# A transformer block on one core: the last 64 features of q and k in 64x64 tiles, a second DMA turn in the attention half, and another order of operations

## The chip, the core and the metric

The kernel runs on one NeuronCore of a Trainium2 chip. The core has a matrix engine (TensorE, PE in the profile, with its weight loads as PEld), three engines for elementwise work (VectorE or DVE, ScalarE or ACT, GpSimd or POOL), and SyncE (SP), which here only issues DMAs. They run side by side and wait for each other by semaphores. PE writes to PSUM, eight banks of 128 partitions by 512 floats, and only DVE and ACT empty these. The metric is the device time of one execution in microseconds; lower is better.

## The reference

Sequence 2048, width 448, batch 1. An attention block with 16 heads of 28 features, in which each position attends to itself and seven earlier positions at distance 2, and then a mixer with a gated MLP; layer norms ahead of each, residuals around each.

```
def _A_ref(x, wqkv, wo):
    H = 16; Dh = D // H
    W, dil = 8, 2
    qkv = (lambda x, *d: x.transpose(*d))((x @ wqkv).reshape(B, S, 3, H, Dh), 2, 0, 3, 1, 4)
    q, k, v = qkv[0], qkv[1], qkv[2]
    ...
    logits = jnp.einsum("bhsd,bhswd->bhsw", q, kg) * scale
    logits = jnp.where(mask[None, None, :, :], logits, -1e9)
    attn = _softmax(logits, axis=-1)
    o = jnp.einsum("bhsw,bhswd->bhsd", attn, vg)
    return (lambda x, *d: x.transpose(*d))(o, 0, 2, 1, 3).reshape(B, S, D) @ wo

def _B_ref(x, w1, w2, w3, w4):
    h = _gelu(_layernorm(x, axis=-1) @ w1)
    ...
    hs = jnp.concatenate([g0, g1, g2, g3], axis=-1) @ w2
    x1 = x + hs
    h2 = _gelu(_layernorm(x1, axis=-1) @ w3) @ w4
    return x1 + h2

h = x + _A_ref(_layernorm(x, axis=-1), A_wqkv, A_wo)
h2 = h + _B_ref(_layernorm(h, axis=-1), B_w1, B_w2, B_w3, B_w4)
```

Here g0 to g3 are the four quarters of h's features, shifted by -1, +1, -2 and +2 positions along the sequence. Everything is bfloat16 with float32 sums in PSUM.

## The kernel before

**Blocks and phases.** The attention half runs over four blocks of 512 rows (index t, four tiles of 128 rows each), the MLP half over five units of 2, 4, 4, 4 and 2 tiles (index u). A phase with its index is a tag: for block t, N1t normalizes, A1t makes q and k, Vt makes v, A2t the products of queries and shifted keys with their sums over features, St the softmax, A3t the weighted sum of values, Ot the output projection with the residual, B1t the second norm, Mt the product with w1 and its gelu. For unit u, B2u is the product with w2, Tu the norm behind it, W3u the product with w3 and its gelu, B3u the product with w4 and the store. The profile writes all of them with one source line, L986, since one helper emits every instruction; groups are told apart by their tiles: `lntm` are normalized rows, `actT` turned rows (features on partitions), `arena` holds weights, q, k and the first mixer product, `qk_r` the query-key products, `bd_r` the block form of the softmax weights, `h3T` the gelu of W3.

**Turning rows.** A product needs its rows with features on the partitions. `TURN` (line 13) says for each block how that is done: "t" by TensorE transposes into PSUM and evictions from there (`transposed`, line 568, and for the first block `transposed_single`, line 589), "d" by one DMA transpose from `lntm` to `actT` on SP's queue (`dma_turn`, line 409). In the attention half it is "ttdd": two blocks by TensorE, two by DMA.

**Two row halves at a time.** The 448 features are cut into chunks of 128 rows at 0, 128, 192 and 320, and the sums run over 64-row halves of them, seven in all. `duo` (line 455) makes two sums at once, in two PSUM banks: matmuls of 64 rows by up to 128 columns alternate between the upper and the lower half of the array, and after half of the work the two sums change places. The second part waits for the end of the first (`sdeps`).

**The last 64 features.** q and k have 448 features each: three groups of 128 and a last one of 64. In A1, the last 64 of q and of k are computed together: POOL gathers their weights side by side into `wr_s` (line 359, filled in `setup_late`, lines 621-622), so that one sum gives 128 columns. The block's 512 rows are split into the two 64-row halves of each tile: bank X has the first halves, bank Y the second, each 128 by 256 with q on the upper 64 partitions and k on the lower. q goes to `qT`, with the first halves on partitions 0-63 and the second on 64-127, and k to `kr[t]` likewise, so four evictions of 64 by 256 follow, and then small ones for the rows that the next window needs. `copy` (line 392) puts an eviction on ACT; unless told otherwise it may be put on DVE instead.

**The order.** Nothing is ordered by the code's sequence. All operations are numbered as they are described, and `ORDER` (line 19) lists the numbers in the order in which they are issued; an engine takes its own operations in that order and waits in it. `OTHER` (line 50) lists the operations that go to their second engine. Waits follow from the data, from reuse of buffers, and from one rule of `arrange`:

```
            if op.insts[0][0] == "dma_start_transpose":
                op.deps.update(turned + moved)
                turned, moved = [op], []
            elif op.is_dma and not callable(op.chan):
                op.deps.update(turned)
                moved.append(op)
```

A DMA transpose waits until the transpose before it and all loads and copies listed since then have landed, and a load or copy waits for the transpose listed last before it. Only the output stores are free of it.

Of the kernel before, what the change touches and what calls it, by code (L numbers as in the profile page):

```python
# [9 lines left out]
F32 = mybir.dt.float32  # L10

_LAST = {}
TURN = {'A1': 'ttdd', 'B1': 'dddd', 'B2': 'tdddd'}
NORM = {'N0': 'vvvv', 'N1': 'avvv', 'B1': 'avvv', 'B2': 'avvvv'}
STATS = {'N1': 'vvva', 'B1': 'avaa', 'B2': 'avvvv'}
NQK, NBD, NLN, NACT, NSM, NO = 3, 4, 2, 4, 1, 6
POWER = {'N1': 'aaaa', 'B1': 'aaaa', 'B2': 'apapp'}
RESIDUAL = 'ttvv'
ORDER = """
# [29 lines left out]
"""  # L49
OTHER = """  # L50
90 94 117 187 447 492 493 505 550 555
"""
FULL = (4,)
FILL = (0, 0, 0, 0)
# [226 lines left out]
def bass_sequential_preLN__sliding_local_dilated__mixer_s_mlp__prompt_kernel(  # L281
    nc, A_x, A_wqkv, A_wo, B_x, B_w1, B_w2, B_w3, B_w4, out,
):
    _, SEQ, D = A_x.shape
# [6 lines left out]
    PADK = 16  # L291
# [6 lines left out]
    S = _Sched()  # L298
# [4 lines left out]
    A_W = A_W3 + 4 * 1792  # L303
# [7 lines left out]
    with ExitStack() as es:  # L311
# [43 lines left out]
        def arv(off, parts, n):  # L355
            return AR[0:parts, off:off + n]

        wqkv_s = arv(A_W, 128, 4 * 1344).rearrange("p (c n) -> p c n", c=4)
        wr_s = arv(A_W + 4 * 1344, 128, 4 * 128).rearrange("p (c n) -> p c n", c=4)
        w3_s = arv(A_W3, 128, 4 * 1792).rearrange("p (c n) -> p c n", c=4)  # L360
        w4_s = arv(A_W, 128, NF * 448).rearrange("p (f n) -> p f n", f=NF)
        qT = arv(A_QG, 128, 4 * QGW).rearrange("p (c n) -> p c n", c=4)
# [29 lines left out]
        def copy(out_ap, in_ap, either=True):  # L392

            if not either:
                return act(out_ap, in_ap, ACT.Copy)
            return S.add("act", "activation", out=out_ap, in_=in_ap, func=ACT.Copy, alts=[("dve", [("tensor_copy", dict(out=out_ap, in_=in_ap))])])
# [56 lines left out]
        TOP, BOT = slice(0, 64), slice(64, 128)  # L453
# [24 lines left out]
        def sums(out, lhsT, rhs, upper):  # L478

            def side(part, chunks):  # L480
                return [(lhsT(c, part), (lambda lo, m, c=c: rhs(c, part, lo, m))) for c in chunks]

            return out, side(TOP, (0, 1, 2, 3) if upper else (0, 1, 3)), side(BOT, (0, 2, 3) if upper else (0, 1, 2, 3))
# [78 lines left out]
        def halves(out, n=4):  # L562
            return lambda v: out(v).rearrange("p (i n) -> p i n", i=n)
# [52 lines left out]
        def setup_late(after):  # L616

            def late(meth, **kw):
                pool(meth, after=after, **kw)

            for lo in (0, 1):
                late("tensor_copy", out=wr_s[:, :, 64 * lo:64 * lo + 64], in_=wqkv_s[:, :, 384 + D * lo:448 + D * lo])
            late("memset", ap=zc[:], constant=0.0)
            for e in range(2):
                late("tensor_copy", out=zc[:, 0:3, e, 16 * e:16 * e + 16], in_=indj[:, 0:3, :])
            late("tensor_copy", out=zc[:, 3, 0, :].rearrange("p (e h) -> p e h", e=2), in_=indj[:, 3:5, :])
            late("memset", ap=onesrow, constant=0.0)
            late("memset", ap=onesrow[0:1, 0:16], constant=1.0)
            late("memset", ap=maskrow, constant=0.0)
            for w in range(1, NW):  # L630
                lo = DIL * (NW - 1 - w)
                late("memset", ap=maskrow[:, 0:64 * w].rearrange("p (r n) -> p r n", n=64)[:, :, lo:lo + DIL], constant=-30000.0)
            late("memset", ap=kk[0][:, :, 0:PADK], constant=0.0)
            late("memset", ap=kr[0][0:64, 0, 0:PADK], constant=0.0)
            late("memset", ap=vw[0:PADK, 0, 0, :], constant=0.0)
            late("memset", ap=gT[:, :, 0:2], constant=0.0)
            late("memset", ap=gT[:, :, 2 + SEQ:4 + SEQ], constant=0.0)
# [30 lines left out]
        def phase_A1(t):  # L668
# [16 lines left out]
            for k in range(0, 6, 2):  # L685
# [2 lines left out]
                ev_a()  # L688
                ev_b()
            X, Y = _Tile(P_bank), _Tile(P_bank)  # L690

            def half(b, at, upper):
                return sums(lambda lo, n: b(halves(lambda v: v[:, 0:256])), lambda c, part: wr_s[part, c, :],
                            lambda c, part, lo, n: a(lambda v: v[part, :, c, at:at + 64]), upper)

            def last(b, lo, n):
                return b(lambda v: v[64:128, 0:256].rearrange("p (j n) -> p j n", j=4)[:, lo:lo + n, 64 - PADK:])

            duo(half(X, 0, True), half(Y, 64, False), ((0, 256),))
            for h, b in enumerate((X, Y)):  # L700
                copy(qT[64 * h:64 * h + 64, 3, now:now + 256], b(lambda v: v[0:64, 0:256]))
                copy(kr[t][64 * h:64 * h + 64, :, PADK:], b(lambda v: v[64:128, 0:256].rearrange("p (j n) -> p j n", j=4)), False)
            copy(kr[t][64:128, :, 0:PADK], last(X, 0, 4), False)
            copy(kr[t][0:64, 1:4, 0:PADK], last(Y, 0, 3), False)
            if t + 1 < NST:
                copy(kr[t + 1][0:64, 0:1, 0:PADK], last(Y, 3, 1), False)
                copy(kk[t + 1][:, :, 0:PADK], kk[t][:, :, 512:KVW])

        def phase_V(t):
# [318 lines left out]
```

## Time and profile before

| | us |
|---|---|
| median of 3 runs | 190.22 |
| range of these runs | 189.76 to 191.77 |
| the profiled execution | 191.08 |
| its span | 189.4 |
| PE busy | 180.2 |
| DVE busy | 129.1 |
| ACT busy | 121.7 |
| POOL busy | 27.7 |

The span is the time from the first to the last instruction that the profiler recorded; 1.7 us of the execution lie around it. Busy time is the union of an engine's instructions; PE's includes matmuls that overlap, so it doesn't say how near PE is to its peak. The granted TensorE clock is 1.00 throughout. In the tables of the profile, a group's line has its source line, engine, operation, written tile <- read tiles, shape and count, then busy us and mean ns of one, then the engine's idle time just before these instructions and what ended it. The page's slices show the two halves of the kernel: DVE and ACT are full for the first part and have room afterwards, while PE is full throughout.

```profile
PE   6899999998998999999799999999999999999994
DVE  6999999999999979999996503963945320100602
ACT  3489999989999799986299397053365014640340
DMA  5991056856905555620932400514007210000213
```

Each digit is a fortieth of the span, 4.7 us, in tenths of busy time.

### The profile page before, as it was taken

Reading aid. Unit: us, or ns where it says so; the run is one execution under the profiler, and the core shown is the slowest. Engines: PE = TensorE matmul, PEld = TensorE weight load, DVE = VectorE, ACT = ScalarE, POOL = GpSimd, SP = SyncE. Lnnn points to the kernel's source line nnn. Section 1 sums busy time; section 2 is a strip of 40 time slices with the busy share of each in tenths; the row PEclk is TensorE's granted clock in tenths of the full one; section 3 lists DMA queues with packets and bytes.
Section 4 is the critical chain, followed back from the end, with each engine's and each line's share of the span. In section 5 each row is a group of like instructions: output and inputs, shape, how many; then the busy total and the mean of one; then the engine's idle time right before and its main releaser. Section 6 shows DMA issues by size and latency. Waiting matters only on the chain.

```text
span 189.4 us, 5659 instructions
## 1 busy us (share of the span) xinstructions
PE 180.2 (95%) x2450; PEld 97.5 (51%) x2450; DVE 129.1 (68%) x227; ACT 121.7 (64%) x293; POOL 27.7 (15%) x61
## 2 busy tenths in 40 slices
PE   6899999998998999999799999999999999999994
PEld 2584433453443654675345455565445554555773
DVE  6999999999999979999996503963945320100602
ACT  3489999989999799986299397053365014640340
POOL 4330000000000000018705000044040660000000
PEclk9999999999999999999999999999999999999999
DMA  5991056856905555620932400514007210000213
GB/s 154 331 294 36 16 111 158 196 102 149 249 1 114 99 171 208 156 78 0 116 83 32 86 0 3 113 37 102 0 18 167 51 37 22 0 3 0 91 60 97
DMA packets 32161, 17.70 MB, mean 93 GB/s; under 512 B 20888, under 2 KB 31624, under 8 KB 32136
## 3 DMA queue, kind: packets, MB, share of 16 engines
q1 hardware_dynamic: 32136, 17.34, 38.1%
q8 instruction: 19, 0.31, 0.7%
q14 instruction: 6, 0.05, 0.1%
HBM read 7.91 MB, written 1.84 MB: 51 GB/s over the span
## 4 chain that ended last, share of the span: by engine, by line
PE 66%; ACT 16%; DVE 8%; DMA 7%; issue 1%; SPq 0%
PE ps L986 66%; DMA actT<-lntm 6%; ACT arena L986 5%; ACT lntm L986 5%; ACT actT L986 3%; ACT vt L986 2%; DVE lntm L986 2%; DVE st L986 2%; DMA xin<-in_A_x_dram 1%; DVE bd_r L986 1%; DVE arena L986 1%; SPq L986 0%; DVE ls L986 0%; DVE mx L986 0%; ACT rs_x L986 0%
## 5 line engine op out<-in xcount | busy, mean ns | idle before, releaser
L986 PE MATMUL ps<-actT,arena 64*128 64x512 bf16 (+1 forms) x756 | 69.8, 329 | 2.0 <-DMA actT<-lntm 1.4
L986 ACT ACTIVATE h3T<-ps 128x512 bf16<-128x512 f32 (+1 forms) x70 | 30.6, 521 | 34.7 <-PE ps L986 34.4
L986 PEld LDWEIGHTS ps<-actT,arena 64*128 64x128 bf16 x756 | 36.2, 94 | 31.4 <-PE ps L986 2.6
L986 PE MATMUL ps<-arena,h3T 64*128 64x448 bf16 (+2 forms) x434 | 45.6, 343 | 0.0
L986 ACT ACTIVATE arena<-ps 128x512 bf16<-128x512 f32 (+6 forms) x71 | 32.2, 491 | 5.5 <-PE ps L986 4.8
L986 DVE SCALAR_TENSOR_TENSOR qk_r<-ps,mrs,arena 128x448 bf16<-128x448 f32 (+1 forms) x17 | 10.7, 652 | 33.7 <-PE ps L986 33.7
L986 PEld LDWEIGHTS ps<-arena,h3T 64*128 64x128 bf16 (+1 forms) x434 | 24.2, 94 | 18.0 <-ACT h3T L986 0.2
L986 DVE TENSOR_TENSOR qk_r<-arena 128x4096 bf16<-128x4096 bf16 (+1 forms) x16 | 32.0, 2013 | 0.0
L986 POOL TENSOR_TENSOR arena<-arena,xin 128x448 f32<-128x448 f32 x16 | 16.7, 1072 | 28.1 <-DVE lntm L986 28.1
L986 DVE TENSOR_TENSOR bd_r<-arena,bmask 80x2048 bf16<-80x2048 bf16 x16 | 19.1, 1213 | 0.0
L986 POOL TENSOR_TENSOR rs_y<-rs_x,mhalf 128x4 f32<-128x4 f32 (+1 forms) x3 | 2.8, 919 | 86.5 <-DVE rs_x L986 86.5
L986 DVE SCALAR_TENSOR_TENSOR arena<-xin,rs_y,ps 128x448 f32<-128x448 bf16 x16 | 10.4, 673 | 6.6 <-PE ps L986 6.5
L986 ACT ACTIVATE lntm<-xin,nm 128x448 bf16<-128x448 bf16 x16 | 10.6, 663 | 6.5 <-DVE nm L986 6.5
L986 PE MATMUL ps<-wo_s,actT 64*128 64x448 bf16 x128 | 14.3, 350 | 0.4 <-ACT actT L986 0.2
L986 PE MATMUL ps<-actT,w_s 64*112 64x512 bf16 x112 | 13.0, 377 | 1.1 <-DMA actT<-lntm 1.1
L986 PE MATMUL ps<-w_s,arena 64*128 64x448 bf16 (+1 forms) x128 | 13.7, 349 | 0.1
L986 ACT ACTIVATE actT<-ps 128x512 bf16<-128x512 f32 (+2 forms) x20 | 12.1, 640 | 1.5 <-PE ps L986 1.4
L986 PE MATMUL ps<-arena,actT 64*128 64x448 bf16 x112 | 12.6, 350 | 0.1
L986 PEld LDWEIGHTS ps<-actT,w_s 64*112 64x112 bf16 x112 | 7.6, 127 | 6.1 <-DMA actT<-lntm 1.6
L986 ACT ACTIVATE rs_x<-mv,epsilon 128x4 f32<-128x4 f32 (+2 forms) x16 | 4.6, 293 | 9.2 <-DVE mv L986 9.1
L986 DVE TENSOR_SCALAR lntm<-xin,nm,rs_y 128x512 bf16<-128x512 bf16 x13 | 4.7, 404 | 8.5 <-ACT rs_y L986 8.5
L986 DVE TENSOR_SCALAR lntm<-arena,mv,rs_y 128x512 bf16<-128x512 f32 x14 | 8.1, 635 | 2.6 <-POOL rs_y L986 2.0
(72 smaller groups left out, 162.1 us busy)
## 6 DMA issues: line engine op xcount, KB each, us to landing
arena<-in_B_w_dram SPq DMA_DIRECT2D x2, 896.0 KB, 6.1
out_dram<-qk_r SPq DMA_DIRECT2D x15, 112.0 KB, 2.0
arena<-in_B_w_dram SPq DMA_DIRECT2D x2, 784.0 KB, 5.2
vw<-vt SPq DMA_DIRECT2D x4, 320.0 KB, 4.8
vw<-vt SPq DMA_DIRECT2D x4, 256.0 KB, 4.3
arena<-in_A_wqkv_dram SPq DMA_DIRECT2D x2, 448.0 KB, 4.4
xin<-in_A_x_dram SPq DMA_DIRECT2D x2, 448.0 KB, 7.0
xin<-in_A_x_dram SPq DMA_DIRECT2D x3, 224.0 KB, 5.3
```

The lines of the kernel that those rows point to most:

```text
L986: inst = getattr(eng, meth)(**kw)
```

## The change

1. In A1, the last 64 features are computed in tiles of 64 rows by 64 columns. Bank X now is q alone and bank Y k alone, each 128 by 256: the first 64-row halves of the tiles on partitions 0-63, the second on 64-127. So four matmuls belong together, one for each quarter of the array: two row halves for the two sums and two column halves for the two halves of the rows. Weights are read from `wqkv_s` directly. Seven such steps make 28 matmuls of 64*64 with 256 columns in a stage, in two groups of 16 and 12, where there were 14 of 64*128, in groups of 8 and 6.
2. Each bank is emptied by one eviction of 128 partitions by 256, and k's may now be put on DVE too. The small evictions stay.
3. `wr_s` and the two POOL copies that fill it are gone.
4. `TURN['A1']` is 'tddd': the second block's rows are turned by a DMA on SP's queue. Its 32 transposes, in four groups, and the two evictions behind them are gone.
5. `ORDER` and `OTHER` are new: 846 numbers instead of 861, and ten operations on their second engine, as before, but others.

```
-TURN = {'A1': 'ttdd', 'B1': 'dddd', 'B2': 'tdddd'}
+TURN = {'A1': 'tddd', 'B1': 'dddd', 'B2': 'tdddd'}
...
-            for lo in (0, 1):
-                late("tensor_copy", out=wr_s[:, :, 64 * lo:64 * lo + 64], in_=wqkv_s[:, :, 384 + D * lo:448 + D * lo])
...
-            def half(b, at, upper):
-                return sums(lambda lo, n: b(halves(lambda v: v[:, 0:256])), lambda c, part: wr_s[part, c, :],
-                            lambda c, part, lo, n: a(lambda v: v[part, :, c, at:at + 64]), upper)
...
-            duo(half(X, 0, True), half(Y, 64, False), ((0, 256),))
-            for h, b in enumerate((X, Y)):
-                copy(qT[64 * h:64 * h + 64, 3, now:now + 256], b(lambda v: v[0:64, 0:256]))
-                copy(kr[t][64 * h:64 * h + 64, :, PADK:], b(lambda v: v[64:128, 0:256].rearrange("p (j n) -> p j n", j=4)), False)
+            both = ((X, D - 64, ((0, 1, 2, 3), (0, 2, 3))), (Y, 2 * D - 64, ((0, 1, 3), (0, 1, 2, 3))))
+            op = None
+            for second in range(2):
+                turned = [op] * second
+                specs = []
+                (bu, wu, cu), (bl, wl, cl) = both[::-1] if second else both
+                for n, (ct, cb) in enumerate(zip(cu[0], cl[1])):
+                    for e in range(2):
+                        for b, w, c, part in ((bu, wu, ct, TOP), (bl, wl, cb, BOT)):
+                            specs.append((e, dict(out=b(lambda v, e=e: v[64 * e:64 * e + 64, 0:256].rearrange("p (i n) -> p i n", i=4)),
+                                                  lhsT=wqkv_s[part, c, w:w + 64], rhs=a(lambda v, e=e, c=c, part=part: v[part, :, c, 64 * e:64 * e + 64]),
+                                                  start=not second and n == 0, stop=bool(second) and n == 2), 256))
+                op = S.group("pe", [("matmul", kw) for _, kw, _ in specs], pe=[(n, "s", None) for _, _, n in specs])
+                op.sdeps.update(turned)
...
+            copy(qT[:, 3, now:now + 256], X(lambda v: v[:, 0:256]))
+            copy(kr[t][:, :, PADK:], Y(lambda v: v[:, 0:256].rearrange("p (j n) -> p j n", j=4)))
```

The first numbers of the old and of the new list:

```
-0 1 39 40 41 42 43 44 6 45 46 47 48 49 5 2 33 8 34 7 9 29 36 10 50 51 12 37 30 13 52 55 56 62 57 53 14 3 58 60 61 63
+8 3 29 9 0 33 1 39 40 41 42 43 44 45 10 46 47 7 5 50 2 55 6 51 48 62 56 57 36 52 60 49 61 58 53 63 54 59 87 64 65 89
```

Where the new list is counted off against the phases, these differences matter for what follows. SP's queue starts with the loads of x and of wqkv as before; then come the second block's DMA turn, a copy of V0's last rows, two loads of wo, another copy of V0, the third block's turn, and only then the remaining loads. DVE takes the first query-key product of A2 in block 0 ahead of the statistics of block 2, which stood ahead of it. Of the evictions that a second engine may take, DVE loses one of A10's turned rows, the small one of q in A10 and one of A13, and takes one more in A32 and one more in A33; of B10's normalizations it takes two instead of one. M1 follows M0 on PE with one group of block 2's softmax between them, and the groups of V3 and A13 that stood there stand ahead of M0. B10's and B11's turns are still neighbours on SP's queue, with a load of w3 and a copy of V2's rows behind them. Three groups of A33 and all of O3 stand behind the first group of M2 on PE, and A33's block products stand behind B12's normalizations on DVE. The attention half's exponentials, logarithms and the gelus change places on ACT ten times instead of eight.

More of the change, by code (lines that the diff above doesn't have):

```diff
@@ L19 @@
 ORDER = """
[29 rows of a table removed]
[28 rows of a table added]
 """
 OTHER = """
-90 94 117 187 447 492 493 505 550 555
+88 182 183 374 477 478 484 490 534 541
 """
@@ L358, in bass_sequential_preLN__sliding_local_dilated__mixer_s_mlp__prompt_kernel @@
         wqkv_s = arv(A_W, 128, 4 * 1344).rearrange("p (c n) -> p c n", c=4)
-        wr_s = arv(A_W + 4 * 1344, 128, 4 * 128).rearrange("p (c n) -> p c n", c=4)
         w3_s = arv(A_W3, 128, 4 * 1792).rearrange("p (c n) -> p c n", c=4)
@@ L690, in phase_A1 @@
             X, Y = _Tile(P_bank), _Tile(P_bank)
-            def half(b, at, upper):
-                return sums(lambda lo, n: b(halves(lambda v: v[:, 0:256])), lambda c, part: wr_s[part, c, :],
-                            lambda c, part, lo, n: a(lambda v: v[part, :, c, at:at + 64]), upper)
-            def last(b, lo, n):
-                return b(lambda v: v[64:128, 0:256].rearrange("p (j n) -> p j n", j=4)[:, lo:lo + n, 64 - PADK:])
-            duo(half(X, 0, True), half(Y, 64, False), ((0, 256),))
@@ L700, in phase_A1 @@
-            for h, b in enumerate((X, Y)):
-                copy(qT[64 * h:64 * h + 64, 3, now:now + 256], b(lambda v: v[0:64, 0:256]))
-                copy(kr[t][64 * h:64 * h + 64, :, PADK:], b(lambda v: v[64:128, 0:256].rearrange("p (j n) -> p j n", j=4)), False)
-            copy(kr[t][64:128, :, 0:PADK], last(X, 0, 4), False)
-            copy(kr[t][0:64, 1:4, 0:PADK], last(Y, 0, 3), False)
+            both = ((X, D - 64, ((0, 1, 2, 3), (0, 2, 3))), (Y, 2 * D - 64, ((0, 1, 3), (0, 1, 2, 3))))
@@ L705, in phase_A1, with last @@
+            def last(lo, h, n):
+                return Y(lambda v: v[64 * h:64 * h + 64, 0:256].rearrange("p (j n) -> p j n", j=4)[:, lo:lo + n, 64 - PADK:])
+            copy(qT[:, 3, now:now + 256], X(lambda v: v[:, 0:256]))
+            copy(kr[t][:, :, PADK:], Y(lambda v: v[:, 0:256].rearrange("p (j n) -> p j n", j=4)))
+            copy(kr[t][64:128, :, 0:PADK], last(0, 0, 4), False)
+            copy(kr[t][0:64, 1:4, 0:PADK], last(0, 1, 3), False)
             if t + 1 < NST:
-                copy(kr[t + 1][0:64, 0:1, 0:PADK], last(Y, 3, 1), False)
+                copy(kr[t + 1][0:64, 0:1, 0:PADK], last(3, 1, 1), False)
```

55 rows, old and new, of the table ORDER are left out of this document.

## The prediction

> **What bounds the kernel now.** I read the busy time of each engine in stretches first, then the chain of waits to see where the stretches end, then the groups by form for prices, then the timeline around the places that the change touches.
>
> ```profile
> 12.40:34.40 22.00, 21.36 (x273) 9.68 (x269) 22.00 (x28) 21.73 (x59) 0.00 (x0) 1.00 0.45 93
> 34.40:61.80 27.40, 25.19 (x506) 11.94 (x506) 26.59 (x38) 26.69 (x71) 0.00 (x0) 1.00 0.58 134
> 61.80:94.40 32.60, 31.02 (x516) 18.17 (x518) 31.21 (x53) 25.20 (x56) 8.00 (x8) 1.00 0.50 120
> 94.40:186.90 92.50, 92.42 (x1066) 51.88 (x1066) 38.58 (x83) 42.28 (x94) 14.51 (x16) 1.00 0.22 49
> ```
>
> Columns: stretch, its length, then busy time (instructions) of PE, weight loads, DVE, ACT, POOL, granted clock 1.00, DMA. Three engines are full together until 61.8, and DVE fullest: 22.00 of 22.00. After 94.4 PE alone is full, and it stays so.
>
> ```profile
> 12.42 1.08 ACT arena L986 x2
> ...
> 15.08 1.83 ACT actT L986 x2
> ...
> 55.81 5.94 DMA actT<-lntm
> ...
> 88.86 5.46 DMA actT<-lntm
> ...
> 94.37 92.46 PE ps L986 x1066
> ```
>
> The chain (start, duration, what) names ACT from 12.42 on, though DVE has no gap there either: of two full engines the chain can show only one. Its last pieces are the frame of my sum. DVE normalizes the second unit of the second half (T1), a DMA turns its rows, W31 starts at 94.37, and PE then runs 92.46 us without a wait. The end moves with W31's start, with PE's work behind it, and with waits that appear there.
>
> **The change, part by part.** *Evictions.* Each of the four stages gives up two of its four 64-partition evictions of the last features, and the second block gives up the two evictions of its transposes.
>
> ```profile
> L986 ACT ACTIVATE h3T<-ps 128x256 bf16<-128x256 f32 x28 | 8.7, 395 | 11.9 <-PE ps L986 11.8
> L986 ACT ACTIVATE arena<-ps 64x256 bf16<-64x256 f32 x15 | 5.7, 377 | 0.3
> L986 ACT ACTIVATE actT<-ps 128x1024 bf16<-128x1024 bf16 x2 | 2.0, 1052 | 0.0
> L986 DVE COPY actT<-ps 128x512 bf16<-128x512 bf16 x3 | 1.3, 418 | 0.2 <-PE ps L986 0.2
> L986 DVE CAST actT<-ps 128x512 bf16<-128x512 f32 x1 | 0.7, 692 | 0.0
> L986 DVE CAST arena<-ps 128x512 bf16<-128x512 f32 x1 | 0.7, 680 | 0.0
> L986 DVE CAST arena<-ps 64x256 bf16<-64x256 f32 x1 | 0.4, 382 | 0.0
> L986 DVE TENSOR_SCALAR lntm<-xin,nm,rs_y 128x512 bf16<-128x512 bf16 x13 | 4.7, 404 | 8.5 <-ACT rs_y L986 8.5
> ```
>
> An eviction of 128 partitions by 256 takes 0.395 us and one of 64 by 256 takes 0.377, so eight calls go for 8 x 0.377 less 8 x 0.018, or 2.9 us, and with the two of 1.05 it is 5.0 us. All of it is ACT's (one of the small ones stood on DVE). ACT's share is worth something only where ACT is what DVE and PE wait for, so I book none of it by itself.
>
> *DVE up to T1.* Here the new order has to be read. Counting the new list off against the phases, DVE's queue up to T1's last normalization loses a copy of A10 (0.42), the small q copy (0.38) and one eviction of A13 (0.68), which all go to ACT; it gains a normalization of B10 (0.40) and an eviction of A32 (0.69). It also puts two operations of S3 behind T1 that stood ahead of it.
>
> ```profile
> 84.25 0.69 DVE L986 TENSOR_REDUCE mx<-ps 128x64 f32<-128x512 f32 x1
> 84.97 0.69 DVE L986 TENSOR_TENSOR ls<-ps,mx 128x512 f32<-128x512 f32 x1
> ```
>
> Sum: -0.42 - 0.38 - 0.68 + 0.40 + 0.69 - 2 x 0.69 = -1.8 us. If DVE stays full, T1's turn is issued at 88.86 - 1.8 = 87.1 and lands, after the same 5.46, at 92.5. The first product of A20 now stands ahead of the statistics of N12, but that only swaps two pieces of a full engine.
>
> *PE up to W31.* The turn is one condition, PE's own arrival the other.
>
> ```profile
> 91.87 1.49 PE L986 MATMUL ps<-arena,h3T 64*128 64x448 bf16 x14
> 94.37 6.43 PE L986 MATMUL ps<-actT,arena 64*128 64x512 bf16 x58 [1.01 <-DMA actT<-lntm]
> 61.80 3.23 PE L986 MATMUL ps<-actT,w_s 64*112 64x512 bf16 x28 [1.09 <-DMA actT<-lntm]
> ```
>
> PE ended its earlier work at 91.87 + 1.49 = 93.36 and then waited 1.01 for the turn; it had waited 1.09 for B10's turn ahead of M0. The prices of what changes:
>
> ```profile
> L986 PE MATMUL ps<-actT,arena 64*128 64x256 bf16 x336 | 21.1, 269 | 0.5 <-DVE bmask L986 0.2
> L986 PE MATMUL ps<-qk_r,zc 128*32 128x512 bf16 x112 | 8.1, 383 | 0.0
> L986 PE MATMUL ps<-ident,lntm 64*128 64x64 bf16 x48 | 1.2, 190 | 0.0
> ```
>
> The busy time over the count is what one instruction adds while others overlap it. The 32 transposes of the second block: 1.2/48 = 25 ns each, -0.8 us. The last features: now 56 matmuls at 21.1/336 = 63 ns, 3.5 us; then 112 of half the columns of weights. No 64x64 tile stands in the trace. Below, the pace of the small transposes, 25 ns, gives 2.8 (-0.7). Above, halves that do not overlap cost 63 each, 7.1 (+3.5). I take the row nearest in kind, the products with column tiles (zc): 8.1/112 = 72 ns for 512 columns, four in flight, so 36 ns for 256: 4.0 us, +0.5.
>
> The eight groups are also a new shape among 64-by-128 ones.
>
> ```profile
> 38.89 0.92 PE L986 MATMUL ps<-arena,actT 64*128 64x448 bf16 x8
> 39.65 0.92 PE L986 MATMUL ps<-wo_s,actT 64*128 64x448 bf16 x8
> 47.66 0.93 PE L986 MATMUL ps<-arena,actT 64*128 64x448 bf16 x8
> 48.52 0.42 PE L986 MATMUL ps<-bd_r,vw 80*32 80x64 bf16 x32
> ```
>
> From start to start eight matmuls took 0.76 us ahead of a group of their own shape and 0.86 ahead of one with column tiles: 0.10 for a change of shape. In the new order the eight groups add eleven such changes (five of sixteen edges touch each other or a column-tiled group that PE would have switched for anyway): +1.1. [...] With shape changes free, PE's sum would be -0.3 instead of +0.8, and W31 would wait for its turn until 92.5.
>
> So PE's work ahead of W31 changes by -0.8 + 0.5 + 1.1 = +0.8. Against it stands the wait of 1.09 at M0: the new order puts fourteen matmuls of V3 and six of A13 ahead of M0 that stood behind it, about 1.7 us (14 at 0.76/8 = 95 ns, 6 at 63), and B10's normalizations stand behind the same DVE work as now. So PE is still busy when that turn lands. PE arrives at 93.36 + 0.8 - 1.09 = 93.1, behind the turn's 92.5. W31 starts at 93.1, which is 1.3 earlier.
>
> *The turned block.* The new DMA stands on SP's queue behind the loads of x. Its issue waits for all of them, and the loads of wo and one wait for V0's rows queue behind it; the next block's turn stands behind those.
>
> ```profile
> xin<-in_A_x_dram SPq DMA_DIRECT2D x2, 448.0 KB, 7.0
> actT<-lntm SPq DMA_TRANSPOSE x10, 4.4
> 5.26 1.38 SPq L986 DMA_DIRECT2D xin<-in_A_x_dram  x2
> 11.76 1.31 DVE L986 TENSOR_SCALAR lntm<-xin,mv,rs_y 128x448 bf16<-128x448 bf16 x4 [0.47 <-ACT rs_y L986]
> 17.07 4.19 PE L986 MATMUL ps<-actT,arena 64*128 64x512 bf16 x42
> ```
>
> The rows are normalized at 13.1; the last load, issued at about 6.2, lands at 13.2 (7.0 later). With 4.4 the turned rows are there at 17.6, 0.5 behind the 17.07 of now; between the loads' contention and an idle queue I keep 16.5 to 19.2 (5.94, the longest above). PE gets V0 and the first product there; DVE, the fullest engine, has the other products of A20 and the statistics of N12 as cover. I cost it at 0; without that cover it is 0.5 to 2.1. The two gathers of weights by POOL, which is idle from 12.4 to 61.8, go for nothing.
>
> *Behind that.* Two places lose cover. M1 follows M0 with little between them, where V3, A13 and B20 stood, and its turn starts only when B10's has landed: 0 to 1.5 us, most of it ahead of W31's other condition. All of O3 (32 matmuls at 95 ns, 3.0 us) and three groups of A33 now stand behind M2's first group, so PE asks for B12's turn that much sooner; DVE's four block products of A33 stand behind B12's normalizations in return: 0 to 1. I take +0.3 for both. ACT gets one more pair of table loads around M3, where it is less than half busy (42.28 of 92.50): 0.
>
> Sum: -1.3 + 0.3 = -1.0 us. The profiled execution took 191.08 us, span 189.4 and 1.7 around it, 0.86 above the median of 190.22. So 190.1 for it, and **189.2** by the median.
>
> **The rivals.**
>
> *The column halves don't overlap (slower).* For it: no row shows two row tiles and two column tiles at once, and twice as many weight loads must hide. [...] Against: four column tiles did overlap (72 ns per 512 columns). Then a matmul costs 63 instead of 36 ns, PE's sum is +3.8 instead of +0.8, W31 starts at 96.1, 1.7 later than now, and with the 0.3 the median is 192.2. It turns slower than before from about 45 ns per matmul: (1.0 + 4.0)/112.
>
> *Nothing reaches the end.* DVE's 1.8 us turn into waits, because its inputs come from PE, which has 0.8 more to do, or from the late turn (2.1 above). For it: the three engines are full together, and relief went to ACT. Against: the two operations of S3 need nothing new to stand behind T1. The median stays at 190.2. That the order simply trades equal pieces is the same case.
>
> *The whole relief counts (faster).* ACT is on the chain from 12.42 on, and 1.83 of its 5.0 us stand in it as one piece. If DVE and PE had been paced by ACT, W31 starts up to 3 us earlier: 187.2. Against: DVE's 22.00 of 22.00.
>
> **How the numbers follow.** Forecast 0.45, halves apart 0.17, nothing reaches the end 0.23, whole relief 0.15. A difference under 1% (1.9 us) is what I call no change. Below 188.3 lies the whole-relief case and a quarter of the forecast's spread (the turn alone would allow 1.8 or more, and the matmuls may cost 25 ns): 0.27. Above 192.1 lie most of the halves case and a part of the late turn together with a lost cover: 0.17. The rest is 0.56. Ends: 187.0, the whole relief, and 192.2, the halves; what goes beyond is left out.
>
> **What would show it.** 112 matmuls of 64*64 at about 36 ns by busy time over count; ACT's busy time near 118 us with DVE's near 129; T1's normalizations ending near 87 and W31 starting near 93, with PE waiting there for no turn; no wait of PE above 1 us at M1, M2, M3 and W32; M0 starting without a wait. I am wrong if W31 starts later than 94.4, or if PE shows waits of over 1 us in total behind it.

## The result and the profile after

The changed kernel took 189.71 us in the median of 19 executions, the kernel before 190.94 in 19 beside them: a ratio of 0.9946, 95% interval 0.9921 to 0.9971. A second measurement (12 executions, first experiment) gave 189.61 and 0.9949 (0.9924 to 0.9973). So it is faster by about 0.5%, 1.0 us. Four of these 31 executions have a mean granted clock of 0.990 or 0.991 and took 191.7 to 192.2; the ratios leave out the three slowest and so aren't the quotients of the medians. The first profile caught the fourth (191.67), with the clock at half for 3.4 us. I therefore read the profile of the second measurement: 189.96 us, span 188.2, clock 1.00, beside 191.08 and 189.4 before.

The end of its chain of waits (start, duration, what):

```profile
62.21 4.28 DMA actT<-lntm
66.51 0.38 SPq L990
66.94 8.46 DMA vw<-vt
75.45 2.76 PE ps L990 x136
78.41 107.32 PE ps L990 x1304
185.75 0.45 DVE qk_r L990
```

Before, the last pieces were T1's normalizations, its turn, and PE from W31 on. Now PE runs without a wait from 78.41, and T1's turn is no longer in the chain: it is issued at 87.42 and has landed by 92.55, when the next DMA, which waits for it, is issued.

```profile
87.42 3.18 SPq L990 DMA_TRANSPOSE actT<-lntm  x1
92.55 0.62 SPq L990 DMA_DIRECT2D vw<-vt  x1
```

The waits of PE on the way there, and W31 (timeline; in brackets the idle time and its releaser):

```profile
38.21 0.70 PE L990 MATMUL ps<-bd_r,vw 80*32 80x64 bf16 x64 [1.11 <-DVE lntm L990]
...
63.20 2.54 PE L990 MATMUL ps<-actT,w_s 64*112 64x512 bf16 x22
...
75.45 0.99 PE L990 MATMUL ps<-bd_r,vw 80*32 80x64 bf16 x96 [0.56 <-DMA vw<-vt]
...
93.08 7.07 PE L990 MATMUL ps<-actT,arena 64*128 64x512 bf16 x64
```

M0 (63.20) and W31 (93.08) start without the 1.09 and 1.01 that stood there. In their place there is a new wait of 1.11 at A30. It is put down to a DVE normalization, which this group doesn't read; in the first profile the same wait is 1.66 and its releaser is the copy of V0's rows (vw<-vt). Another wait, of 0.56, is for V2's rows, which stand behind B11's turn on SP's queue.

The kernel before and then the changed one, in two stretches up to W31 (length, then busy time of PE, weight loads, DVE, ACT and POOL with instructions, granted clock, DMA share, GB/s):

```profile
12.40:61.80 49.40, 46.54 (x779) 21.62 (x775) 48.59 (x65) 48.43 (x128) 0.00 (x0) 1.00 0.52 116
61.80:94.37 32.57, 31.00 (x514) 18.14 (x515) 31.18 (x53) 25.17 (x56) 8.00 (x8) 1.00 0.50 120
```

```profile
12.40:61.80 49.40, 46.98 (x809) 21.11 (x803) 48.53 (x66) 44.49 (x122) 0.00 (x0) 1.00 0.55 122
61.80:93.08 31.28, 30.36 (x510) 18.41 (x506) 28.74 (x53) 25.33 (x59) 17.32 (x10) 1.00 0.59 138
```

ACT gave up 3.9 us ahead of 61.8; DVE is as full as ever there. From 12.40 to W31 PE's busy time went from 77.54 to 77.34 and its idle time from 4.43 to 3.34: together the 1.29 by which W31 starts earlier.

### The profile page after: what moved, and what is told of

Its sections match the earlier page's. It is cut to its first block, busy times and chain, and to the rows that moved or that the text cites. A ratio compares the mean times of both kernels' runs of the same rounds, so it can differ in the third digit from the quotient of the medians.

```text
span 190.0 us, 5698 instructions
## 1 busy us (share of the span) xinstructions
PE 181.6 (96%) x2474; PEld 99.8 (53%) x2474; DVE 127.2 (67%) x227; ACT 119.2 (63%) x285; POOL 33.9 (18%) x59
## 4 chain that ended last, share of the span: by engine, by line
PE 80%; DMA 9%; DVE 5%; issue 2%; SPq 2%; ACT 1%
PE ps L990 80%; DMA vw<-vt 4%; DVE qk_r L990 3%; DMA arena<-in_A_wqkv_dram 3%; DMA actT<-lntm 2%; SPq L990 2%; ACT arena L990 1%; DVE st L990 1%; DVE lntm L990 1%; DVE mx L990 0%; DVE mv L990 0%; DVE nm L990 0%; SPq L988 0%
## 5 line engine op out<-in xcount | busy, mean ns | idle before, releaser
L990 PE MATMUL ps<-actT,arena 64*128 64x512 bf16 (+2 forms) x812 | 69.5, 326 | 1.2 <-DMA arena<-in_A_wqkv_dram 0.5
L990 PEld LDWEIGHTS ps<-actT,arena 64*128 64x128 bf16 (+1 forms) x812 | 38.0, 96 | 28.9 <-issue 2.1
L990 ACT ACTIVATE arena<-ps 128x512 bf16<-128x512 f32 (+6 forms) x65 | 29.5, 506 | 8.6 <-PE ps L990 8.3
L990 POOL TENSOR_TENSOR mrs<-nm,rs_y 128x4 f32<-128x4 f32 x4 | 9.7, 2436 | 54.5 <-ACT rs_y L990 54.5
L990 PE MATMUL ps<-wo_s,actT 64*128 64x448 bf16 x128 | 15.2, 364 | 0.1
L990 PE MATMUL ps<-arena,actT 64*128 64x448 bf16 x112 | 13.7, 366 | 0.2
L990 ACT ACTIVATE actT<-ps 128x512 bf16<-128x512 f32 (+1 forms) x17 | 9.4, 600 | 4.1 <-PE ps L990 4.0
L990 DVE BATCH_NORM_STATS2 st<-xin 128x6 f32<-128x448 bf16 x16 | 9.0, 613 | 1.6 <-DMA xin<-in_A_x_dram 1.6
L990 ACT ACTIVATE vt<-ps 128x448 bf16<-128x448 f32 x16 | 8.7, 551 | 2.0 <-PE ps L990 1.9
L990 PEld LDWEIGHTS ps<-wo_s,actT 64*128 64x128 bf16 x128 | 6.3, 97 | 6.9 <-PE ps L990 0.9
```

The costliest lines, as they stand in the source:

```text
L990: inst = getattr(eng, meth)(**kw)
```

## The experiments

All are orders or code of these two kernels with one thing altered. In diffs of an order only the neighbours of what moved are shown.

**The changed kernel again** (a_again), unaltered.

> The changed kernel, unaltered. In its profiled execution the granted clock stood near 0.5 from 40 to 43.4 us and the span was 190.0; other executions had the clock at 1.00 and spans of 187.2 to 188.4. My theory (the low clock is an accident of some executions, and costs about 2 us where it falls): executions at clock 1.00 take 189.0 to 190.1 us, any at 0.99 take 191.5 to 192.2; in a profile at clock 1.00 W31 starts at 92.0 to 93.1 without a wait of PE, T1's normalizations end at 86.5 to 87.5, and DVE has no gap of 0.9 and 1.5 us between 41 and 45. Rival (the low clock costs nothing, something else makes the long executions long): spans of both kinds at clock 1.00.

189.61 us. Eleven executions at clock 1.00 took 189.03 to 190.36, the one at 0.991 took 191.95. My theory holds, but for the 190.36, which lies above its 190.1. W31 starts at 93.08 without a wait, at the late end of what I expected, T1's normalizations end at 87.2, and the gaps of 0.9 and 1.5 us on DVE are gone.

**The parts in the old order.** The tiles alone (b_tiles): the change to the code of A1's tail, none to TURN or the sequence, apart from the numbers that disappear. The turn alone (b_turn):

```diff
-TURN = {'A1': 'ttdd', ...
+TURN = {'A1': 'tddd', ...
```

Both (b_both): the two together, still in the old sequence.

> The kernel before with the 64x64 tiles alone: its order kept, the two gathers and eight small evictions left out. My theory (ACT's relief is worth nothing by itself, only DVE's queue and PE's arrival count): DVE gives up one eviction of 0.38, PE takes on 112 x 41 ns less 56 x 63 ns = 1.1 us and some changes of shape (up to 1.6) of which up to 2.1 us fall into its waits ahead of M0 and W31: -0.4 to +0.6 us, ratio 0.998 to 1.003. Rival (ACT paced the first 60 us): ACT gives up 2.5 us ahead of M0, ratio 0.985 to 0.992. Rival (the new tiles cost more than their waits hide): ratio above 1.005.

> The kernel before with the second block turned by DMA alone: its order kept, but the turn stands on SP's queue ahead of the first two loads of wo. My theory (DVE is full and has cover, the turn lands at 17.6 instead of the rows being there at 17.07): 0 to +0.5 us, ratio 1.000 to 1.003. Rival (ACT's 1.83 us in the chain of waits at 15.08 counts): ratio 0.990 to 0.993. Rival (the late rows reach DVE): +0.5 to +2.1 us, ratio 1.003 to 1.011.

> The kernel before with both changes to the code, the 64x64 tiles and the turn by DMA, in its old order. Theory A (the old order has no use for ACT's relief, so the parts' prices add up; the tiles alone gave +1.4 and the turn alone +0.5): 191.4 to 192.4 us. Theory B (ACT's relief counts once it is large enough, 5.0 us): 188.0 to 189.8 us.

Tiles 191.84 us, ratio 1.0062 (1.0028 to 1.0095); turn 190.89, 1.0020 (0.9994 to 1.0046); both 192.23, 1.0072 (1.0045 to 1.0098). The turn alone came out as expected. For the tiles alone the third case came in, which I hadn't favoured; its profiled execution (190.88) lies below its own median and doesn't show what the others lost. For b_both, theory A held: the two prices add up, and in its profile T1's normalizations start at 86.08, no earlier than the 85.58 before, so no gain from ACT's relief shows on DVE.

The profiles of these three runs show one thing more. T1's turn lands 4.27 us after its issue in each of them, instead of 5.46, and W31 starts at 92.93 (tiles), 92.53 (turn) and 93.70 (both), earlier than the 94.37 before. After its first 16 matmuls PE then waits 0.82 us for a bank that DVE empties. In the old order an early turn alone therefore meets this bank as the next condition.

**The new order without the parts.** Either part undone in the changed kernel: the 64x128 tiles back (a_oldtail; each extra eviction directly behind the one it belonged to), the transposes back (a_oldturn; where the DMA stood), and both (a_order). In a second try the transposes stand directly behind the last normalization (a_oldturn2).

> The new order alone: the last features in 64x128 tiles with four evictions of 64 partitions and the two gathers, the second block turned on TensorE, everything in the new order (the eight extra evictions behind the ones they belonged to). Theory A (the order alone brings the gain: on DVE's queue T1's normalizations no longer meet the two additions of POOL, so its turn is out of the way, and PE's new arrangement does the rest): 189.0 to 190.0 us, the same as the changed kernel. Theory B (the new order lives on the relief of ACT, 5.0 us, since it hands ACT three copies more; without it ACT is late and PE waits): 190.6 to 193 us, with new waits of PE for ACT's evictions ahead of M0.

> The changed kernel with the 64x128 tiles for the last features again (four evictions of 64 partitions, two gathers), the second block still turned by DMA. Theory A (PE paces from 78 us on, and the small tiles cost it 112 x 41 less 56 x 63 ns = 1.1 us): 188.5 to 189.4 us, faster than the changed kernel. Theory B (ACT's 2.9 us are needed by the new order): 190.0 to 191.5 us.

> The changed kernel with the second block turned on TensorE again (32 transposes and two evictions of 1.05 us on ACT), the 64x64 tiles kept. Theory A (the turn by DMA gains nothing, its rows come 0.5 us later instead): 189.3 to 190.0 us. Theory B (PE's 0.8 us and ACT's 2.1 us count): 190.4 to 192.5 us.

> As the changed kernel with the second block turned on TensorE, but with the 32 transposes and their two evictions directly behind the block's last normalization in the order, and not where the DMA stood (there the evictions stood behind ACT's work for the third block, and PE idled 3.85 us for them). Theory A (what the turn by DMA takes off, PE's 0.8 us and ACT's 2.1 us, is used by the new order): 190.4 to 192.1 us. Theory B (only the place of the evictions cost time): 189.3 to 190.0 us.

All four are slower, as theory B says, and each by more than its range. As a table, with the ratio to the kernel before:

| code | old order | new order |
|---|---|---|
| old | 190.4 to 191.3 (1) | 197.79 (1.0334) |
| 64x64 tiles | 191.84 (1.0062) | 195.65 and 195.60 (1.0215, 1.0237) |
| turn by DMA | 190.89 (1.0020) | 194.31 (1.0168) |
| both | 192.23 (1.0072) | 189.61 (0.9949) |

The old code is the kernel before, given as its medians beside the different runs. Where PE waits in the new order without the parts (a_order):

```profile
24.67 4.26 PE L985 MATMUL ps<-actT,arena 64*128 64x512 bf16 x22 [5.22 <-ACT actT L985]
39.29 0.49 PE L985 MATMUL ps<-ident,pb 64*80 64x64 bf16 x16 [1.19 <-ACT arena L985]
```

and with the turn by DMA but the old tiles (a_oldtail):

```profile
20.54 1.69 PE L985 MATMUL ps<-actT,arena 64*128 64x512 bf16 x14 [1.06 <-ACT arena L985]
...
32.77 0.49 PE L985 MATMUL ps<-ident,pb 64*80 64x64 bf16 x16 [0.88 <-ACT arena L985]
```

In a_order PE waits for evictions by ACT, and the clock stands at 0.50 for 6.8 us, which is part of the loss (see the end). In a_oldtail, whose profiled execution took 192.99 us at clock 1.00 throughout, these waits explain little: PE starts the transposes of T0's rows at 77.31, where the changed kernel starts them at 77.26. Of the 3.1 us by which its span is longer (191.3 and 188.2), 2.8 are one wait behind that:

```profile
80.63 0.61 PE L985 MATMUL ps<-qk_r,zc 128*32 128x512 bf16 x8 [2.79 <-issue]
```

"issue" means that the profile shows nothing that PE waited for; the cause stays open. What goes from the code is mostly ACT's time, worth nothing in the old order, and the new order has handed ACT other work in its place. That it stands only with that time free is my reading, which the waits for ACT support where the turn is put back (5.22 us in a_order, 3.85 in a_oldturn), and which isn't shown for the tiles. The places of the put-back operations are mine; another search might lose less. a_oldturn2 shows at least that the late transposes of a_oldturn weren't its only trouble.

**Two tiles or four in flight** (a_halves).

```diff
-                for n, (ct, cb) in enumerate(zip(cu[0], cl[1])):
-                    for e in range(2):
+                for e in range(2):
+                    for n, (ct, cb) in enumerate(zip(cu[0], cl[1])):
```

> The changed kernel with the 28 matmuls of each stage's last features issued one column half after the other instead of alternating, so that at most two tiles are in flight. Theory A (the alternation is what brings 41 ns apiece): 55 to 65 ns apiece by busy time over count, 1.6 to 2.7 us more of PE, 190.5 to 192.2 us. Rival (the order within the group doesn't matter): 41 ns and 189.6 us.

189.50 us, 4.8 us for the 112 matmuls, 43 ns apiece: my theory fell. The single starts in the trace say why (us; one group in the second half of its run, the changed kernel and a_halves):

```
alternating:      30.303 30.306 30.309 30.383   30.412 30.415 30.419 30.491
half after half:  30.699 30.727 30.750 30.758   30.808 30.836 30.859 30.867
```

Four start every 0.108 us in both. Two tiles alone would give two: of the 64*128 tiles with the same 256 columns, which alternate between the upper and the lower half, two start every 0.109 us in the kernel before (78.056 and 78.060, then 78.166 and 78.169). So matmuls of the second half seem to start ahead of earlier ones of the first. The trace doesn't name the half of a start, but the distances fit: in a_halves the second pair of a group starts 26 to 31 ns behind the first where eight matmuls of one half are listed first, and 20 where six are, about 3.3 ns for each matmul in between, as between neighbours; with alternation it is 7. The pace is 27 ns, and the 41 of busy time over count hold the run-out of short groups.

**T1's normalizations and POOL** (b_pool). DVE's part of the new order, first the kernel before, then the changed one:

```profile
85.58 3.25 DVE L986 TENSOR_SCALAR lntm<-arena,mv,rs_y 128x512 bf16<-128x512 f32 x4
```

```profile
85.30 1.91 DVE L990 TENSOR_SCALAR lntm<-arena,mv,rs_y 128x512 bf16<-128x512 f32 x4 [0.92 <-POOL rs_y L990]
```

The same four instructions take 1.34 us less. What ran beside them on POOL, before and after:

```profile
85.42 2.21 POOL L986 TENSOR_TENSOR arena<-arena,xin 128x448 f32<-128x448 f32 x2
```

```profile
76.85 2.03 POOL L990 TENSOR_TENSOR arena<-arena,xin 128x448 f32<-128x448 f32 x2 [4.55 <-ACT lntm L990]
```

These are T0's additions. The experiment moves nothing but them, in the kernel before (550 and 549 are T0's normalizations, 610 T1's reciprocal roots):

```diff
-... 550 ... 549 ... 610 ... 552 ... 551 ...
+... 550 ... 549 551 552 ... 610 ...
```

> The kernel before with one change of order: the two additions that POOL does for T0 stand directly behind T0's normalizations, and no longer beside T1's. Theory A (POOL's additions, which run from 85.4 to 87.6 in the kernel before, are what stretches T1's four normalizations to 3.25 us; in the changed kernel they take 1.91 us): 1.8 to 2.1 us for the four, T1's turn issued at 87.3 to 87.8, no wait of PE at W31's first matmul, and 0.3 to 1.0 us off the time, since a wait for a bank may follow at the next group. Rival (the additions slow DVE's work at 77 to 79 us by as much): T1's normalizations begin 1 us later, the time as before.

189.97 us, ratio 0.9955 (0.9929 to 0.9980). DVE and PE of this run:

```profile
85.46 1.91 DVE L986 TENSOR_SCALAR lntm<-arena,mv,rs_y 128x512 bf16<-128x512 f32 x4
```

```profile
93.36 6.43 PE L986 MATMUL ps<-actT,arena 64*128 64x512 bf16 x58 [0.65 <-DMA actT<-lntm]
```

Theory A held in duration and time, and the rival fell: the additions now run at 76.69, and T1's normalizations begin at 85.46, no later than before. The wait at W31 didn't go, though: the turn was issued at 87.40 as expected but took 5.9 us to land instead of the 5.5 and 5.1 of the other two, and no wait for a bank came behind it. With no change to the code, this one move gives as much as the whole change, within the intervals.

**The wait at A30.** Two ways to free V0's copies (129, 130). Ahead of the third block's turn (321), a_vw:

```diff
-... 236 131 231 ... 321 242 22 ... 129 ... 23 ... 130 ...
+... 236 131 129 130 231 ... 321 242 22 ... 23 ...
```

and behind that turn, but ahead of the last two loads of wo (22, 23), a_wo:

```diff
-... 321 242 22 ... 129 ... 23 ... 130 ...
+... 321 242 ... 129 ... 130 22 23 ...
```

> The changed kernel with V0's two large copies of rows issued ahead of the third block's turn instead of behind it. Theory A (PE's idle time at 37 to 39 us, which is a wait for these copies, lets the clock fall, and the wait itself costs nothing because DVE is the fuller engine there): the wait of 1.66 us at A30 goes, no execution shows a clock below 0.995, and the median stays with the undisturbed executions of the changed kernel, 189.6 +- 0.3. Rival B (the wait itself is on the path): about 1.7 us less than those, 188.0. Rival C (the copies only delay the turn behind them, which becomes a new wait at A12): up to 1.5 us more, 191.0.

> The changed kernel with the last two loads of wo issued behind V0's two large copies of rows instead of ahead of each of them; the third block's turn stays where it is. Theory A (from 38 us on PE is the engine that paces, with under 1 us of waits up to W31, so its wait of 1.11 us for these copies counts): the copies are issued 0.4 and 1.0 us earlier, the wait falls under 0.4 us, 188.6 to 189.1 us, and executions with the clock below 0.995, 4 of 31 so far, become rarer. Theory B (DVE, full to 36.9 and beyond, paces there): the wait falls and others take its place, 189.3 to 189.9 us.

a_vw: 190.81 us, 1.0023 (0.9990 to 1.0056), rival C: the turn waits until the copies have landed and is issued at 27.87 instead of 25.70, and PE, at its next groups of A12, waits behind ACT:

```profile
32.39 2.53 PE L991 MATMUL ps<-actT,arena 64*64 64x256 bf16 x24 [2.18 <-ACT vt L991]
```

a_wo: 188.78 us, 0.9908 (0.9878 to 0.9938), six executions all at clock 1.00. Theory A, although the wait only went down to 0.65. W31 starts 1.2 us earlier than in the changed kernel: about 0.5 is this wait, 0.6 the wait for V2's rows, which is gone as well, and 0.2 stood there ahead of the copies.

```profile
37.54 0.70 PE L991 MATMUL ps<-bd_r,vw 80*32 80x64 bf16 x64 [0.65 <-DVE lntm L991]
...
91.86 7.07 PE L991 MATMUL ps<-actT,arena 64*128 64x512 bf16 x64
```

This is the fastest version by its median. It wasn't timed beside the changed kernel on one chip, and their intervals against the kernel before overlap; of its executions 5 of 6 took 189.18 or less, of the changed kernel's 4 of 31.

## Why the prediction was right, and where its steps failed

The forecast of 189.2 us (a ratio of 0.9946) came out at 189.7 and 0.9946; the base of 190.22 was the median of three executions and low, and the difference, forecast at -1.0, is -1.2 and -0.8 in the two measurements. W31, forecast at 93.1, starts at 93.08, and PE from there to its last matmul takes 92.65 instead of 92.46 (the 0.3 for lost cover is 0.2). The profiled execution, forecast at 190.1, took 189.96. The frame was right: W31 starts earlier because PE no longer waits ahead of M0 and for T1's turn. But two terms behind 93.1, PE's work (-0.2 instead of +0.8) and its waits (-1.1 instead of -2.1), were off by 1 us each and cancelled, so that W31 agrees so closely is luck; and T1's turn came in time by another way than mine.

- *The new order on DVE's queue, -1.8, T1's turn issued at 87.1.* Issued at 87.42, for another reason. Up to the start of T1's normalizations DVE works 81.33 us before and 79.82 now, 1.5 less, so the work went about as counted; that DVE would stay full is what failed. Of the 1.5, 0.8 lies ahead of 12.40 (the two copies of A10), where the next normalizations start at 11.74 instead of 11.76 all the same. From 12.40 on DVE works 0.7 less and waits 0.4 more, so T1's normalizations start only 0.28 earlier. There is a new wait of 0.92 for POOL's reciprocal roots: the two operations of S3 that moved away had filled this time, and POOL's product took longer.

```profile
84.43 1.03 POOL L986 TENSOR_TENSOR rs_y<-rs_x,mhalf 128x4 f32<-128x4 f32 x1 [73.23 <-DVE rs_x L986]
```

```profile
83.33 1.93 POOL L990 TENSOR_TENSOR rs_y<-rs_x,mhalf 128x4 f32<-128x4 f32 x1 [4.45 <-DVE rs_x L990]
```

  The rest is the duration of the normalizations, 1.34. I had counted which operations stand on which queue and priced each by its own row, and not asked what runs beside it on another engine. b_pool shows that in the old order this alone carries 0.8 us. In the new one, by an estimate, the turn would have landed 1.34 later without it, at 93.9, 0.8 behind PE.
- *Eleven changes of shape, +1.1.* This step failed. A change does cost what I took: in the changed kernel's first group, the next four of the same shape start 0.099 behind the last of four (12.424 to 12.523), and the next shape 0.201 behind it (12.533 to 12.734), so 0.10. But I counted only the edges of the eight new groups, not those that the new sequence takes away among the others. Counted over single matmuls up to W31, the shape (48 rows taken as 64) changes 46 times before and 51 times now: the new groups bring 14 changes, and nine of the others go. So it is five, or +0.5. And the price by busy time over count already holds the run-out of a group, so part of it may have been booked twice.
- *PE's other work: -0.8 and +0.5.* Right in the sum. The rows of the changed kernel:

```profile
L990 PE MATMUL ps<-actT,arena 64*128 64x256 bf16 x280 | 16.9, 269 | 0.6 <-DVE bmask L990 0.4 <-issue 0.2
L990 PE MATMUL ps<-actT,arena 64*64 64x256 bf16 x112 | 4.6, 276 | 0.1
L990 PE MATMUL ps<-ident,lntm 64*128 64x64 bf16 x16 | 0.4, 191 | 0.0
```

  16.9 + 4.6 - 21.1 is +0.4, and 0.4 - 1.2 is -0.8. Within the +0.4, the new tiles took 4.6 instead of 4.0, and the 280 others 16.9 instead of the 17.6 that stayed in my sum. PE's busy time from 12.40 to W31 changes by -0.2 instead of +0.8; with five changes of shape the terms would give +0.1, and the last 0.3 is open.
- *The waits at M0 and W31, -2.1.* They went. At M0 the reason fits the forecast: B10's turn has landed by 62.21, when B11's is issued, and PE then still works on V3 for 1.0 us; no run moves those groups alone. But 1.0 came back elsewhere, mostly as the 1.11 at A30. The prediction named the queue (the loads of wo and the next turn behind the new DMA) and didn't follow it to V0's copies, which here stand between those loads. a_wo, where this wait is 0.5 shorter and the one for V2's rows goes too, is 0.8 us faster.
- *ACT's 5.0 us, not booked.* Right for this sum: b_both has the same relief in the old order and is 0.7% slower. It left out that the new order hands ACT other work: ACT's busy time fell by only 2.4, from 121.7 to 119.3. Without the relief the same order is 1.7 to 3.3% slower than the kernel before, though part of that is the clock's and, in a_oldtail, the wait without a releaser.
- *The turned block at no cost.* The rows came as computed (issued at 13.19; the next DMA, which waits for it, at 17.63), and alone it cost +0.2%, which includes zero. The tiles, without the order, did cost something, 0.6%.
- *The rivals.* Halves that don't overlap: four matmuls of 64x64 start every 0.108 us, 27 ns apiece. The whole relief: it doesn't reach the end directly. Nothing reaches the end: refuted by W31's start.

## What to carry to other kernels

An order is fitted to the code that it was found for, so the parts of such a change can't be priced one by one: here the parts alone gain nothing (+0.6% and +0.2%), the order without them loses, and together they gain. When a queue's work is summed, look at what runs beside each piece as well as what stands ahead of it: T0's two additions on POOL, moved away from T1's normalizations, were worth as much as the whole change. And when a DMA is added to a fenced queue, follow the queue to the last transfer that someone waits for.

## What the runs showed of the hardware

**DVE beside POOL.** Four normalizations of 128x512 from float32 take 3.25 us beside POOL's additions in the kernel before and 3.26 in b_both; without them 1.91 in the changed kernel and in b_pool, 1.92 in a_wo. Of POOL's 2.2 us, 1.34 come on top of DVE's. It may go the other way, too: in the changed kernel a small product of 128x4 occupied POOL for 9.14 us beside a full DVE, mostly products for qk_r and bd_r (63.12), and 0.21 beside an eviction by DVE (91.26). No run isolates this.

**The clock.** TensorE's granted clock fell to 0.50 during or after some of PE's idle times of 1.66 to 5.22 us. Windows of the first profile of the changed kernel (behind the length stands PE's busy time; the clock is the third number from the end):

```profile
36.00:37.00 1.00, 1.00 (x20) 0.36 (x20) 1.00 (x2) 0.87 (x2) 0.00 (x0) 1.00 0.72 152
37.00:38.00 1.00, 0.18 (x4) 0.00 (x0) 1.00 (x3) 0.00 (x0) 0.00 (x0) 1.00 0.94 176
38.00:39.00 1.00, 0.15 (x21) 0.18 (x25) 1.00 (x4) 0.00 (x0) 0.00 (x0) 1.00 0.34 72
39.00:40.00 1.00, 1.00 (x70) 0.64 (x59) 1.00 (x4) 0.66 (x2) 0.00 (x0) 1.00 0.03 11
40.00:41.00 1.00, 1.00 (x10) 0.43 (x8) 1.00 (x1) 1.00 (x3) 0.00 (x0) 0.53 0.07 16
41.00:42.00 1.00, 1.00 (x8) 0.40 (x6) 0.12 (x2) 1.00 (x3) 0.00 (x0) 0.50 1.09 128
42.00:43.00 1.00, 1.00 (x8) 0.45 (x6) 1.00 (x2) 0.40 (x1) 0.00 (x0) 0.50 0.87 173
43.00:44.00 1.00, 1.00 (x12) 0.44 (x8) 0.76 (x1) 0.00 (x0) 0.00 (x0) 0.77 1.03 223
```

PE idles for 1.66 us, works on for 1.2, and then has half the clock for 3.4 us. The span is 190.0 us against the 188.2 at full clock. In a_vw an idle time of 2.18 us was followed by the same 3.4 us at half clock, in a_order one of 5.22 us had 6.8 us at half clock, from within it on; but in a_oldtail one of 2.79 us was followed by none. The changed kernel is hit in 4 of 31 executions. What sets the 3.4 us, and which executions are hit, no run here shows. Whether a_wo, with its shorter wait, is free of it can't be told from six executions.
